# Splitting the opening loads of a GEGLU kernel over two DMA queues: transposes on SyncE, weights on ScalarE

## The chip, the cores and the metric

One core of a Trainium2 chip runs the kernel. The metric is device time in microseconds (us), lower is better. The runs of the kernel before lie between 275.07 and 275.65 us. Each run is marked fast or slow by its time against the fastest of the same kernel; ratios use fast runs alone.

Names of engines: PE is TensorE (matrix products), PEld its weight loads, DVE is VectorE, ACT is ScalarE, POOL is GpSimd, SP is SyncE. "ACTq" and "SPq" are the DMA issues of ScalarE and SyncE. The profile calls SyncE's DMA queue q1 and ScalarE's q10. A load is issued by an engine and lands when all its data have arrived; a semaphore, a counter that the load raises then, tells of it.

## The reference

```python
B, S, D, F = 32, 32, 1024, 3584          # 1024 tokens
return (gelu(x @ w_gate) * (x @ w_up)) @ w_down      # all bf16
```

## The kernel before

The kernel computes `x @ w_gate` and `x @ w_up` in chunks of 256 columns, with x transposed so that its columns lie on the partitions. The change concerns only the first 20 us, the "head", in which the first data arrive. x comes in two ways: a small piece untransposed (`x_nat`, turned on TensorE), and four DMA transposes (`load_xT`). The weights come as plain loads. `DT` is 8 tiles of 128 along D, `KD` is 4 and `KQ` is 2.

```python
load_nat(nc.sync, 0, 0, HALF)
load_nat(nc.scalar, 0, HALF, NB_P)
...
load_ahead(0, 0, 1)                       # a12a rows k0: 128 KB of w_gate, SyncE
load_nat(nc.scalar, 1, 0, NB_P)
load_ahead(0, 1, 2, nc.scalar)            # a12a k1
for which, eng in enumerate((nc.sync, nc.scalar)):
    load_w(eng, 0, which, KD, KD + KQ)    # wg and wu d4-5
load_xT(0, KD + KQ, DT)                   # T1: 256 KB transpose
load_ahead(0, KQ, KD)                     # a12a k2-3: 256 KB
load_w0(nc.sync, KD + KQ, DT)             # wg, wu d6-7: 128 KB each
load_ahead(1, 0, KD)                      # second a12a: 512 KB
load_xT(0, 0, KD)                         # T2: 512 KB transpose
load_w0(nc.sync, 0, KD)                   # wg, wu d0-3: 256 KB each
load_xT(1, 0, KD)                         # T3: 512 KB transpose
load_xT(1, KD, DT)                        # T4: 512 KB transpose
```

TensorE uses them in this order:

```python
# a12a k0-1 (psC/psA), then:
plain0(tok0, KD, KD + KQ)                 # wg, wu d4-5
for j, copy in enumerate((nc.scalar.copy, nc.vector.tensor_copy) * 2):
    product_ahead(ps[j], 0, j, KQ)        # a12a k2-3 and T1
    copy(ahead[0][:, j, :], ps[j])
plain0(tok0, KD + KQ, DT)                 # wg, wu d6-7
...                                       # chunk 1's loads are issued
for j, tag in enumerate("CCAA"):
    product_ahead(ps, 1, j)               # second a12a
    ...
# then wg, wu d0-3 with T2, later T3 and T4
```

The framework gives every load one of eight semaphores in turn, and a load waits until the load that had its semaphore before has landed. The traces show such waits (before: 0.3 us of SyncE for `x_nat`, ahead of wu d6-7).

Of the kernel before, what the change touches and what calls it, by code (L numbers as in the profile page):

```python
# [13 lines left out]
def kernel(  # L14
# [20 lines left out]
    nc = tc.nc  # L35
# [13 lines left out]
    DT, FT = D // P, F // P  # L49
    KD = DT // 2  # L50
# [3 lines left out]
    KQ = DT // 4  # L54
# [76 lines left out]
    def load_w(eng, ci, which, d0, d1):  # L131
        f0 = ci * FC * P
        src = (wg_r, wu_r)[which]
        eng.dma_start(out=w_tiles[ci, which][:, d0:d1, :], in_=src[:, d0:d1, f0 : f0 + FC * P])
# [54 lines left out]
    with tc.manual_schedule():  # L189
# [12 lines left out]
        def load_ahead(i, k0, k1, eng=nc.sync):  # L202
            f0, n = FC + i * KB, min(KB, NAHEAD - i * KB)
            eng.dma_start(
                out=a12_ahead[i][:, k0:k1, : n * P],
                in_=wg_r[:, KD + k0 : KD + k1, f0 * P : (f0 + n) * P],
            )

        def load_w0(eng, d0, d1):
            for which in (0, 1):  # L210
                load_w(eng, 0, which, d0, d1)

        def load_xT(nb, d0, d1):
            t = ((b11, b12), (b21, b22))[d0 // KD][nb]
            nc.sync.dma_start_transpose(
                out=t[:, d0 % KD : (d1 - 1) % KD + 1, :], in_=xf[nb * NB : (nb + 1) * NB, d0 * P : d1 * P]
            )
# [3 lines left out]
        load_ahead(0, 1, 2, nc.scalar)  # L221
        for which, eng in enumerate((nc.sync, nc.scalar)):
            load_w(eng, 0, which, KD, KD + KQ)
        load_xT(0, KD + KQ, DT)
        load_ahead(0, KQ, KD)
        load_w0(nc.sync, KD + KQ, DT)
        load_ahead(1, 0, KD)
        load_xT(0, 0, KD)
        load_w0(nc.sync, 0, KD)
        load_xT(1, 0, KD)  # L230
        load_xT(1, KD, DT)

# [17 lines left out]
        def plain(ps, which, fl, nb, d0, d1, first=0, last=DT - 1):  # L250
            for dt in range(d0, d1):
                nc.tensor.matmul(  # L252
                    ps,
                    lhsT=w_tiles[0, which][:, dt, fl * P : (fl + 1) * P],
                    rhs=x_rows(dt, nb),
                    start=(dt == first),
                    stop=(dt == last),
                )
# [24 lines left out]
        def product_ahead(ps, i, j, k0=0, k1=KD, cols=slice(None)):  # L283
            for k in range(k0, k1):
                nc.tensor.matmul(  # L285
                    ps[:, cols],
                    lhsT=a12_ahead[i][:, k, j * P : (j + 1) * P],
                    rhs=b21[:, k, cols],
                    start=(k == 0 and not cols.start),
                    stop=(k == KD - 1),  # L290
                    skip_group_check=True,
                )
# [4 lines left out]
        def plain0(tok0, d0, d1):  # L297
            for which in (0, 1):
                for dt in range(d0, d1):
                    for fl in range(FC):  # L300
                        plain(tok0[fl][which], which, fl, 0, dt, dt + 1, KD, KD - 1)
# [11 lines left out]
        for j, copy in enumerate((nc.scalar.copy, nc.vector.tensor_copy) * 2):  # L313
            product_ahead(ps[j], 0, j, KQ)
            copy(ahead[0][:, j, :], ps[j])
        plain0(tok0, KD + KQ, DT)
        a12_ahead.append(xpool.tile([P, KD, (NAHEAD - 2 * KB) * P], bf16, name="a12b"))
        load_w_all(1, 1)
# [297 lines left out]
```

## Time and profile before

| what | before | where it is read |
|---|---|---|
| time | 275.38 us, median of 3 | runs |
| span, PE busy | 273.3 us, 267.9 us | page, engines |
| DMA wait of PE in the head | 0.54 us, at 4.45 us | timeline of PE |
| DMA rate, 4 to 8 us and 8 to 12 us | 279 and 288 GB/s | table of windows |

Two lines of the page of the kernel before: the busy time of PE with its share of the span, and the chain of work that ended last, by engine.

```profile
PE 267.9 (98%) x1190; PEld 188.9 (69%) x1206; DVE 196.6 (72%) x196; ACT 110.8 (41%) x181; POOL 108.3 (40%) x55
...
PE 97%; DMA 1%; issue 0%; ACT 0%; SPq 0%
```

TensorE is the bound, from its first product to the end. A wait of TensorE in the head goes straight into the total.

The timeline of PE before, at the first use of each later load (start in us, duration, engine, line, operation, output and inputs, shape, count). A bracket at the end would name a wait.

```profile
8.48 1.03 PE L285 MATMUL psC<-b,a12a 128*128 128x512 bf16 x4
...
10.21 0.81 PE L252 MATMUL psA<-b,wg 128*128 128x512 bf16 x3
11.07 1.03 PE L252 MATMUL psB<-b,wu 128*128 128x512 bf16 x4
11.94 1.89 PE L285 MATMUL psC<-b,a12a 128*128 128x512 bf16 x8
...
15.39 1.03 PE L252 MATMUL psA<-b,wg 128*128 128x512 bf16 x4
16.25 1.03 PE L252 MATMUL psB<-b,wu 128*128 128x512 bf16 x4
...
25.75 1.89 PE L270 MATMUL psA<-b,wg 128*128 128x512 bf16 x8
```

No bracket: nothing is waited for. The DMA view of the kernel before, asked for single issues, gives size and time from issue to landing. Here are a12a k2-3 (issued at 3.60 us), wg d6-7 (4.21), the second a12a (5.44) and T2 (5.96).

```profile
a12a<-in_w_gate_dram SPq DMA_DIRECT2D x1, 256.0 KB, 4.5
...
wg<-in_w_gate_dram SPq DMA_DIRECT2D x1, 128.0 KB, 4.3
...
a12a<-in_w_gate_dram SPq DMA_DIRECT2D x1, 512.0 KB, 5.1
...
b<-in_x_dram SPq DMA_TRANSPOSE x1, 6.2
```

Issue plus landing time gives 8.1, 8.5, 10.5 and 12.2 us, each ahead of its use (8.48, 10.21, 11.94 and, for T2, 15.39 us). The table of windows before, for 4 to 8 us and 8 to 12 us (stretch, length, busy time of PE, PEld, DVE, ACT and POOL, granted clock, DMA share, GB/s):

```profile
4.00:8.00 4.00, 3.55 (x26) 2.55 (x27) 0.74 (x4) 0.12 (x1) 0.00 (x0) 1.00 1.22 279
8.00:12.00 4.00, 3.95 (x19) 1.83 (x19) 1.38 (x2) 1.17 (x2) 0.00 (x0) 1.00 1.13 288
```

The DMA engines are at full share.

### The profile page before, as it was taken

What the parts mean: (1) busy time and instruction counts of PE and PEld (TensorE: products, weight loads), DVE (VectorE), ACT (ScalarE), POOL (GpSimd) and SP (SyncE); (2) the same over time, 40 slices, a digit from 0 to 9 for tenths busy, and PEclk for the clock granted to TensorE, in tenths of its full rate; (3) what the DMA queues carried; (4) which work ended last, traced back from release to release, by engine and by line L of the source; (5) the groups of instructions that cost most, each with busy time, mean ns of one, the idle gap of its engine ahead of it and who ended that gap; (6) DMA issues with size and microseconds to landing.
All of it is one profiled execution on the core that took longest, in us unless ns stands there. A gap on an engine that the chain in (4) does not pass through costs nothing.

```text
span 273.3 us, 3350 instructions
## 1 busy us (share of the span) xinstructions
PE 267.9 (98%) x1190; PEld 188.9 (69%) x1206; DVE 196.6 (72%) x196; ACT 110.8 (41%) x181; POOL 108.3 (40%) x55
## 2 busy tenths in 40 slices
PE   8999999999999999999999999999999999999995
PEld 4444777877778676676868686754447888888883
DVE  1269996877756676776667576568999999999611
ACT  1271664554643646455563636430300032972001
POOL 1000099997897694949576684000000000000000
PEclk9999999999999999999999999999999999999999
DMA  7994321414505405050514280004992254786202
GB/s 166 290 251 105 111 75 40 117 42 113 156 11 143 137 19 155 0 153 0 156 28 126 79 269 1 0 2 132 329 342 83 93 175 163 240 279 203 78 0 78
DMA packets 53841, 33.77 MB, mean 124 GB/s; under 512 B 9792, under 2 KB 53824, under 8 KB 53824
## 3 DMA queue, kind: packets, MB, share of 16 engines
q1 hardware_dynamic: 50304, 31.00, 39.3%
q10 hardware_dynamic: 3520, 2.56, 2.9%
q8 instruction: 9, 0.15, 0.3%
q14 instruction: 8, 0.07, 0.1%
HBM read 29.62 MB, written 2.10 MB: 116 GB/s over the span
## 4 chain that ended last, share of the span: by engine, by line
PE 97%; DMA 1%; issue 0%; ACT 0%; SPq 0%
PE psA L270 34%; PE psA L446 18%; PE psC L270 17%; PE psC L446 7%; PE psB L446 7%; PE psB L270 5%; PE psB L252 3%; PE psA L252 2%; PE psC L285 2%; PE psA L285 1%; DMA a12a<-in_w_gate_dram 1%; ACT o_sb L586 0%; SPq L191 0%; PE tp L243 0%
## 5 line engine op out<-in xcount | busy, mean ns | idle before, releaser
L270 PE MATMUL psA<-t,s 128*128 128x512 f32 x208 | 54.2, 402 | 0.0
L262 ACT ACTIVATE h<-c 128x512 bf16<-128x512 f32 x52 | 31.6, 627 | 36.6 <-DVE c L350 36.6
L270 PEld LDWEIGHTS psA<-t,s 128*128 128x128 f32 x208 | 39.1, 188 | 9.2
L168 POOL TENSOR_TENSOR s<-wu 128x1024 fp32r<-128x1024 bf16 x12 | 27.4, 2285 | 23.7 <-PE psC L270 12.8
L350 DVE TENSOR_TENSOR c<-sn,psA 128x512 f32<-128x512 f32 x26 | 17.8, 684 | 16.8 <-PE psA L270 16.8
L270 PEld LDWEIGHTS <-wg 128*128 128x128 bf16 x168 | 15.4, 98 | 20.1 <-issue 3.4
L169 POOL TENSOR_TENSOR s<-s,wg 128x1024 fp32r<-128x1024 f32 x12 | 27.7, 2312 | 0.9
L171 POOL TENSOR_TENSOR s<-wg,wu 128x1024 fp32r<-128x1024 bf16 x12 | 26.6, 2216 | 0.0
L355 ACT COPY sn<-psA 128x512 f32<-128x512 f32 x42 | 23.6, 584 | 6.8 <-PE psA L270 6.8
L355 ACT COPY sn<-psC 128x512 f32<-128x512 f32 x26 | 15.2, 588 | 26.9 <-PE psC L270 22.8
L270 PE MATMUL psA<-t,a22r 128*128 128x512 f32 x104 | 25.9, 391 | 0.0
L270 PE MATMUL psC<-t,s 128*128 128x512 f32 x104 | 25.8, 390 | 0.0
L270 PE MATMUL psC<-b22r,s 128*128 128x512 f32 x104 | 25.7, 389 | 0.0
L270 PE MATMUL psA<-b,wg 128*128 128x512 bf16 x100 | 24.1, 379 | 0.2
L270 PEld LDWEIGHTS psC<-t,s 128*128 128x128 f32 x104 | 19.4, 188 | 4.4 <-ACT ahead L377 0.3
L270 PEld LDWEIGHTS psA<-t,a22r 128*128 128x128 f32 x104 | 19.5, 188 | 4.1
L270 PEld LDWEIGHTS psC<-b22r,s 128*128 128x128 f32 x104 | 19.5, 188 | 4.1
L350 DVE TENSOR_TENSOR c<-sn,psC 128x512 f32<-128x512 f32 x26 | 17.7, 688 | 5.5 <-PE psC L270 5.5
L369 DVE TENSOR_TENSOR hi<-h,psA 128x512 bf16<-128x512 bf16 x14 | 9.6, 689 | 12.5 <-PE psA L270 12.5
L425 DVE TENSOR_TENSOR hi<-c,h 128x512 bf16<-128x512 f32 x14 | 18.0, 1284 | 0.5
L425 DVE TENSOR_TENSOR lo<-c,h 128x512 bf16<-128x512 f32 x12 | 17.8, 1479 | 0.6
L170 POOL TENSOR_TENSOR s<-wg,s 128x1024 fp32r<-128x1024 bf16 x8 | 17.3, 2156 | 0.6
(94 smaller groups left out, 396.9 us busy)
## 6 DMA issues: line engine op xcount, KB each, us to landing
wdb<-in_w_down_dram SPq DMA_DIRECT2D x12, 512.0 KB, 5.0
wu<-in_w_up_dram SPq DMA_DIRECT2D x11, 512.0 KB, 4.0
wdb<-in_w_down_dram SPq DMA_DIRECT2D x12, 384.0 KB, 4.7
wg<-in_w_gate_dram SPq DMA_DIRECT2D x6, 512.0 KB, 5.1
wg<-in_w_gate_dram SPq DMA_DIRECT2D x10, 256.0 KB, 4.4
v<-in_w_down_dram SPq DMA_DIRECT2D x4, 512.0 KB, 6.7
out_dram<-o_sb ACTq DMA_DIRECT2D x16, 128.0 KB, 1.7
v<-in_w_down_dram SPq DMA_DIRECT2D x4, 384.0 KB, 7.6
```

The lines of the kernel that those rows point to most:

```text
L168: yield eng.tensor_tensor(s1, a21, a22, ADD)
L169: yield eng.tensor_tensor(s2, s1, a11, SUB)
L170: yield eng.tensor_tensor(s4, a12, s2, SUB)
L171: yield eng.tensor_tensor(s3, a11, a21, SUB)
L252: nc.tensor.matmul(ps, lhsT=w_tiles[0, which][:, dt, fl * P : (fl + 1) * P], rhs=x_rows(dt, nb), start=(dt == first), stop=(dt == last),)
L262: nc.scalar.activation(h, src, ACT.Gelu_apprx_tanh)
L270: nc.tensor.matmul(ps, lhsT=lhs[:, k, :], rhs=rhs[:, k, :], start=(start and k == 0), stop=(k == KD - 1), skip_group_check=True,)
L350: tt(t, s, ps, ADD)
L355: nc.scalar.copy(t, ps)
L369: tt(g_of(ft)[:, :NB], h0, psa, MUL)
L425: tt(g_of(ft)[:, NB:], added(sn5[fl], psa[fl]), h1[fl], MUL)
L446: nc.tensor.matmul(banks[m], lhsT=lhs(k)[:, m * P : (m + 1) * P], rhs=rhs(k), start=(start and k == 0), stop=(k == HF - 1), skip_group_che ...
```

## The change

Its intent: after its first three loads SyncE issues only the transposes of the head, whose issue is long, and the weights no longer queue behind them. ScalarE, idle early on, issues the weights.

```diff
         for which, eng in enumerate((nc.sync, nc.scalar)):
             load_w(eng, 0, which, KD, KD + KQ)
+
         load_xT(0, KD + KQ, DT)
-        load_ahead(0, KQ, KD)
-        load_w0(nc.sync, KD + KQ, DT)
-        load_ahead(1, 0, KD)
+        load_ahead(0, KQ, KD, nc.scalar)
+        load_w0(nc.scalar, KD + KQ, DT)
+        load_ahead(1, 0, KD, nc.scalar)
         load_xT(0, 0, KD)
-        load_w0(nc.sync, 0, KD)
         load_xT(1, 0, KD)
         load_xT(1, KD, DT)
...
             product_ahead(ps[j], 0, j, KQ)
             copy(ahead[0][:, j, :], ps[j])
+        load_w0(nc.scalar, 0, KD)
         plain0(tok0, KD + KQ, DT)
```

## The prediction

> **What bounds the kernel.** TensorE. The page gives PE 267.9 us busy of a 273.3 us span (98%), and the chain of waits is 97% PE. From 4.45 us on, the timeline shows no PE gap over about 0.05 us in the head. Its only DMA wait is 0.54 us for the first `a12a` rows at 4.45 us, plus start-up before it; the change touches neither. So nearly nothing can be gained: at most some 0.5 us.
>
> **What the change does.** It removes no bytes and no PE work. Five loads (`a12a` k2-3 256 KB, `wg`/`wu` 128 KB each, second `a12a` 512 KB; then `wg`/`wu` 256 KB each) move from the SyncE to the ScalarE queue. On SyncE they took 0.37 to 0.58 us of issue each; the transposes took 1.34, 4.23 and 4.96 us (for two). SyncE thus finishes its transposes some 3 us earlier (13 instead of 16.4 us) and chunk 1's weights are issued earlier. ScalarE gets about 2 us of issues in an idle stretch: its table load slips from 2.83 to about 5 us, done before its first copy at 9.12 us. The last `wg`/`wu` are issued after its copy at 9.98 us, so about 10.6 and 11.1 us against 10.23 and 10.86.
>
> **Where it touches the critical path.** In the table of 1 us windows the DMA engines are at full share from 4 to 18 us, at 180 to 350 GB/s. Before, one queue held the order of need. Issue time plus time to landing, against PE's first use:
> - `a12a` k2-3: lands 8.1, used 8.27
> - `wg` / `wu` d6-7: 8.5 / 8.9, used 9.99 / 10.86
> - second `a12a`: 10.55, used 11.72
> - first half of x (transposed): 12.2; `wg` / `wu` d0-3: 13.7 / 14.55, used 15.18 / 16.04
> - second token half: 16.6 and about 18.5, used 18.84 and 22.3
>
> Slack is only 0.2 to 1.9 us. Now 1.5 MB of transposes needed at 15 us or later are in flight beside 1 MB of weights needed before 12 us. The Trainium skill, "DMA: Bandwidth & Descriptors", section "Issuing engines are not separate DMA queues", says the DMAs of both queues run on the same 16 engines and interleave, and that a second issuer saves only issue time. The trace agrees in the one overlap it has: ScalarE's `wu` (issued 2.35) landed at 6.55, SyncE's transpose (issued 2.21) at 7.3[...].
>
> Estimate with equal shares (some 145 GB/s each, from the 290 GB/s of the windows) from 6.4 us: `a12a` k2-3 at 8.2, `wg`/`wu` at 9.0/9.9, second `a12a` at about 13.5 instead of 10.55, a stall of up to 1.8 us at 11.7 us. If weights get a bigger share (their rows are 512 or 1024 bytes, transposed rows 256), it lands near 11.8 and hardly stalls. The later `wg`/`wu` land at 15 to 17 us; a stall at 11.7 absorbs that. Lateness does not add up: the largest counts. All of it reaches the end, since PE is full afterwards. Transposes and chunk 1 weights arrive earlier, which pays nothing.
>
> **Prediction.** 276.3 us (+0.9). Range 275.0 to 278.2. Faster by over 2%: 0.01; within 2%: 0.95; slower by over 2%: 0.04.
>
> **What would show it.** PE waiting on DMA at the products of the second `a12a` (about 11.7 us) for 0.5 to 2 us, its landing time up from 5.1 to 7 us or more; transposes of the first x half landing near 10 us, not 12.2; SyncE issuing chunk 1's `wu` near 13 us; the rest of the timeline shifted by one constant; PE busy time unchanged.
>
> **What would make it wrong.** Transposes that hold up the other queue's descriptors altogether (then several us, even over 2%); weights favoured in the sharing (then no change); a ScalarE issue blocked so long that its copies come late.

## The result, and the profile after

The changed kernel took 278.25 us, median of 4 (277.94 to 278.94), beside 275.5 us for the kernel before in the same rounds. The ratio is 1.0106, with a 95% interval of 1.0083 to 1.0129. A ratio here is the mean time of one kernel's fast runs over that of the other's of the same rounds, so it is not quite the ratio of the medians. In microseconds it is 0.0106 x 275.5 = 2.9. Below, "+2.9 us" always means a ratio turned into us that way.

The same two lines of the page after:

```profile
PE 268.6 (97%) x1190; PEld 188.3 (68%) x1206; DVE 195.3 (71%) x196; ACT 110.9 (40%) x181; POOL 108.2 (39%) x55
...
PE 92%; DMA 6%; ACTq 0%; issue 0%; ACT 0%
```

PE has the same work (268.6 against 267.9 us), but the chain now holds 6% of DMA. The timeline of PE after, at the same places:

```profile
8.97 1.04 PE L285 MATMUL psC<-b,a12a 128*128 128x512 bf16 x4
...
12.34 0.82 PE L252 MATMUL psA<-b,wg 128*128 128x512 bf16 x3 [1.47 <-DMA wg<-in_w_gate_dram]
13.22 1.03 PE L252 MATMUL psB<-b,wu 128*128 128x512 bf16 x4
14.39 1.90 PE L285 MATMUL psC<-b,a12a 128*128 128x512 bf16 x8 [0.15 <-DMA a12a<-in_w_gate_dram]
...
17.86 1.03 PE L252 MATMUL psA<-b,wg 128*128 128x512 bf16 x4
19.05 1.04 PE L252 MATMUL psB<-b,wu 128*128 128x512 bf16 x4 [0.17 <-DMA wu<-in_w_up_dram]
...
28.55 1.89 PE L270 MATMUL psA<-b,wg 128*128 128x512 bf16 x8
```

Subtracting row from row gives the delay so far:

| first use of | before | after | delay so far |
|---|---|---|---|
| a12a k2-3 | 8.48 | 8.97 | 0.49 |
| wg d6-7 | 10.21 | 12.34 | 2.13 |
| second a12a | 11.94 | 14.39 | 2.45 |
| wg d0-3 | 15.39 | 17.86 | 2.47 |
| wu d0-3 | 16.25 | 19.05 | 2.80 |
| first product of chunk 1 | 25.75 | 28.55 | 2.80 |

The spans differ by 2.9 us, so nearly the whole loss (2.80 us) arises before 19.1 us. More than half of it (1.64 us) arises at wg d6-7. (A bracket counts only PE's idle time; matrix products are pipelined and their ends modelled, so the delays of starts are the better measure.)

The DMA view after, for the same four loads, now issued at 3.17 (a12a k2-3), 4.55 (wg d6-7), 5.50 (second a12a) and 3.60 us (T2):

```profile
a12a<-in_w_gate_dram ACTq DMA_DIRECT2D x1, 256.0 KB, 5.8
...
wg<-in_w_gate_dram ACTq DMA_DIRECT2D x1, 128.0 KB, 7.7
...
a12a<-in_w_gate_dram ACTq DMA_DIRECT2D x1, 512.0 KB, 8.8
...
b<-in_x_dram SPq DMA_TRANSPOSE x1, 11.0
```

They land at 8.9, 12.3, 14.4 and 14.6 us. ScalarE issued wg d6-7 and the second a12a within 0.35 us of when SyncE had issued them before (4.21 and 5.44). Nothing was won in issue time, and landing takes 3.4 to 3.7 us longer. T2, issued 2.4 us earlier than before, lands 2.4 us later. The table of windows after:

```profile
4.00:8.00 4.00, 3.34 (x25) 2.29 (x26) 0.73 (x4) 1.28 (x1) 0.00 (x0) 1.00 1.21 182
8.00:12.00 4.00, 2.73 (x12) 0.89 (x10) 1.38 (x2) 1.17 (x2) 0.00 (x0) 1.00 1.23 227
```

The engines are as busy as before (1.21 and 1.23) but move 182 and 227 GB/s, not 279 and 288. The DMA view after, for 5 to 11 us, by queue (packets, MB, share of 16 engines):

```profile
q1 hardware_dynamic: 3023, 0.77, 92.0%
q10 hardware_dynamic: 530, 0.38, 33.8%
```

SyncE's transposes got 0.77 MB through, ScalarE's more urgent weights 0.38 MB. Last, three lines of the chain of waits after, in order of time (start, length, what):

```profile
5.50 8.85 DMA a12a<-in_w_gate_dram
14.35 0.02 issue
14.37 4.63 DMA wu<-in_w_up_dram
```

ScalarE issued wu d0-3 only when the second a12a had landed, because the two have one semaphore (the trace has them under one number). I had expected that issue at 11.1 us.

One more stretch shows how the two queues were served. From 11 to 13 us SyncE's T3 (issued at 8.70 us) and ScalarE's second a12a (issued before it, at 5.50 us) were both under way. The DMA view for these 2 us, by queue:

```profile
q10 hardware_dynamic: 744, 0.55, 114.1%
q1 hardware_dynamic: 29, 0.01, 1.7%
```

The load issued later moved next to nothing. That is no fixed share per queue. Nor do transposes always start so late: in m1's stretch A, below, 0.17 MB had moved 2.1 us after the issue of the first one.

### The profile page after: what moved, and what is told of

It is laid out like the page before. It is cut to its first block, busy times and chain, and to the rows that moved or that the text cites. A ratio compares the mean times of both kernels' runs of the same rounds, so it can differ in the third digit from the quotient of the medians.

```text
span 276.2 us, 3351 instructions
## 1 busy us (share of the span) xinstructions
PE 268.6 (97%) x1190; PEld 188.3 (68%) x1206; DVE 195.3 (71%) x196; ACT 110.9 (40%) x181; POOL 108.2 (39%) x55
## 4 chain that ended last, share of the span: by engine, by line
PE 92%; DMA 6%; ACTq 0%; issue 0%; ACT 0%
PE psA L270 34%; PE psA L447 18%; PE psC L270 17%; PE psC L447 7%; PE psB L447 7%; PE psB L270 5%; DMA a12a<-in_w_gate_dram 3%; PE psB L252 2%; DMA wu<-in_w_up_dram 2%; PE psA L252 2%; DMA x_nat<-in_x_dram 1%; PE psC L285 1%; ACTq L134 0%; ACT o_sb L587 0%; ACTq L191 0%
## 5 line engine op out<-in xcount | busy, mean ns | idle before, releaser
L270 PEld LDWEIGHTS <-wg 128*128 128x128 bf16 x168 | 15.4, 98 | 20.2 <-issue 3.4
L426 DVE TENSOR_TENSOR hi<-c,h 128x512 bf16<-128x512 f32 x14 | 16.6, 1188 | 0.5
```

Of the source, the lines that this page charges most:

```text
L270: nc.tensor.matmul(ps, lhsT=lhs[:, k, :], rhs=rhs[:, k, :], start=(start and k == 0), stop=(k == KD - 1), skip_group_check=True,)
L426: tt(g_of(ft)[:, NB:], added(sn5[fl], psa[fl]), h1[fl], MUL)
```

## The experiments

The theory after the result, called F: both queues feed the same engines, and a load is served roughly by its time of issue across both. The change lets T2, needed at 15.4 us, be issued at 3.6 us, ahead of wg, wu and the second a12a (4.55 to 5.5 us), which are needed by 12 us. Part M of the theory (then F+M): transposes in flight beside plain loads of the other queue lower the total rate.

Rivals. S, from the prediction: the two queues share equally, whatever was issued first. L: the waits of ScalarE's issues for earlier landings. T: the late issue of the last wg/wu. G: any two queues lose rate. All but the three marked "wrong" are correct.

| run | what | against before, 95% interval | in us |
|---|---|---|---|
| e1_head_only | first four weight loads moved | 1.0065 to 1.0117 | +2.5 |
| e2_tail_only | last two moved | 1.0022 to 1.0062 | +1.2 |
| e3_gated | the change, T2 held back to 6 us | 1.0099 to 1.0222, unclear | see there |
| e4_one_queue_late | one queue, T2 put before wg | 1.0034 to 1.0068 | +1.4 |
| e5_gated_tail_back | e3 with the last two on SyncE | 0.9998 to 1.0044 | +0.6 |
| e6_plain_after (wrong) | the change, plain copies for transposes | 1.0108 to 1.0140 | +3.4 |
| e7_plain_before (wrong) | before, plain copies for transposes | 1.0000 to 1.0044 | +0.6 |
| m1_queues (wrong) | loads alone, by kind and queue | none | none |
| r_after_again | the changed kernel again | 1.0073 to 1.0143 | +3.0 |
| e8_merged_head | e1 with merged first loads | 1.0024 to 1.0085 | +1.5 |
| e9_merged_before | before with merged first loads | 1.0054 to 1.0113 | +2.3 |

### e1: the first four loads alone

```diff
 # against the changed kernel
         load_xT(0, 0, KD)
+        load_w0(nc.sync, 0, KD)
         load_xT(1, 0, KD)
...
-        load_w0(nc.scalar, 0, KD)
         plain0(tok0, KD + KQ, DT)
```

> Half of the change: the first four weight loads go to the ScalarE queue, the last two (wg/wu d0-3) stay on SyncE between the transposes. Theory F (order of issue: the second transpose of x, issued at 3.6 us, is served before wg, wu and the second a12a issued at 4.55 to 5.5 us): most of the loss stays, +2.0 to +2.8 us, wg d6-7 lands near 12 us. Rival T (the late issue of the last wg/wu on ScalarE at 12.8 and 14.4 us): loss gone or under +0.8 us.

It took +2.5 us, and the view of waits has this line for PE (total, times, longest):

```profile
PE psA L253 <- DMA wg<-in_w_gate_dram: 1.4, 1, 1.4
```

Wg d6-7 landed at 12.2 us. The first four loads alone bring most of the loss, as F said; T is not the main cause.

### e2: the last two loads alone

```diff
 # against the kernel before
-        load_w0(nc.sync, 0, KD)
...
+        load_w0(nc.scalar, 0, KD)
         plain0(tok0, KD + KQ, DT)
```

> The other half: the first four loads stay on SyncE ahead of the second transpose, only the last wg/wu go to ScalarE between its copies. Theory F: wg d6-7 lands near 8.5 us as before, total 0 to +0.8 us. Rival T: +1.5 us or more.

Wg d6-7 landed at 8.1 us and was not waited for. The run took +1.2 us, over the 0.8 that F allowed. Its one large wait:

```profile
PE psB L251 <- DMA wu<-in_w_up_dram: 1.2, 1, 1.2
```

That is the same fault at another place. SyncE, rid of these two loads, issued T3 at 9.9 us and T4 at 11.9 us. ScalarE's wu d0-3 came at 12.0 us, beside T4, and took 5.2 us to land instead of 3.7. One of its six runs (282.0 us) was slow. The two halves (2.5 and 1.2) do not add up to 2.9: a delay at wg d6-7 gives the later loads more time.

### e3 and e5: T2 held back

```diff
 # e3, against the changed kernel
         load_ahead(1, 0, KD, nc.scalar)
+        nc.gpsimd.tensor_copy(b11[:, 0, :1], a12_ahead[0][:, 1, :1])   # T2 overwrites this column
         load_xT(0, 0, KD)
 # e5, against e3
+        load_w0(nc.sync, 0, KD)
         load_xT(1, 0, KD)
...
-        load_w0(nc.scalar, 0, KD)
```

The copied column makes T2 wait for an early load; T2 then overwrites it, and the result is right.

> The changed kernel with one thing more: the second transpose waits (through a one-column GpSimd copy) for the second a12a row block, which landed at 6.05 us, so it is issued near 6.3 us, after ScalarE has issued wg, wu and the second a12a (4.55 to 5.5 us). The result stays right. Theory F (order of issue decides): wg d6-7 and wu land near 8.5 to 9.5 us, second a12a near 10.5 to 11.5, the 1.5 us stall is gone, total +0.2 to +1.0 us over before. Rival S of the prediction (two queues share the engines equally, whatever was issued first): transposes still take half, second a12a lands at 13 us or later, total +1.5 us or more. Rival L (the waits of ScalarE's issues for earlier landings): nothing changes, +2.5 us or more.

> The gated kernel of e3 with its last two weight loads (wg/wu d0-3) back on SyncE. Two queues remain for the first four loads, but no transpose is issued in their midst and no load of ScalarE falls beside the later transposes. Theory F+M (what hurts is a transpose issued ahead of a needed load, and transposes in flight beside loads of the other queue, which together move 160 to 210 KB/us instead of 290): both are gone, so the time is near that of before, 0 to +0.8 us, no stall over 1 us. If it stays at +1.5 us or more, the second queue hurts in a way the theory does not hold.

The total of e3 missed the expectation of F: four of its six runs were slow, 281.8 to 282.8 us, and the two counted as fast lie 4 us apart (277.6 and 281.5). The profiled run was slow, so I draw nothing from its total and leave its scatter unexplained. In e5, which keeps the gate and only takes e2's fault out, the profile is of a fast run. T2 was issued at 5.8 us, after the second a12a (5.4 us), and wg d6-7 landed at 8.3 us, the second a12a at 10.6 us, against 8.5 and 10.5 in the kernel before. The windows of e5, 4 to 8 and 8 to 12 us:

```profile
4.00:8.00 4.00, 3.91 (x27) 2.50 (x28) 0.74 (x4) 1.28 (x1) 0.19 (x1) 1.00 1.17 296
8.00:12.00 4.00, 4.00 (x21) 1.77 (x19) 1.38 (x2) 1.17 (x2) 0.00 (x0) 1.00 1.12 269
```

The rate is back at 296 and 269 GB/s, PE is busy throughout, and the time is +0.6 us with an interval that touches zero. Four weight loads still go through ScalarE. e5 is e1 with the one gating line more, and that line takes +2.5 us to +0.6. So neither the second queue as such (nor L: ScalarE's loads still wait for landings, wu d6-7 and the second a12a are issued at 5.0 and 5.4 us as in the changed kernel) costs the time; T2's place in time does. The gate has a side effect: wg d6-7 takes over another semaphore and is issued at 3.5 us, not 4.2 as in e1; wu d6-7 and the second a12a are not moved forward by it. The DMA view of e5 for 7 to 9 us, with T2 issued (5.8 us) behind these two:

```profile
q10 hardware_dynamic: 878, 0.59, 114.8%
q1 hardware_dynamic: 27, 0.00, 0.8%
```

Again the load issued later stood back. So an unequal but fixed share of the queues, a rival that I had not named, is out too. e5 is no faster than before.

### e4: the same order on one queue

```diff
 # against the kernel before
         load_ahead(0, KQ, KD)
+        load_xT(0, 0, KD)
         load_w0(nc.sync, KD + KQ, DT)
         load_ahead(1, 0, KD)
-        load_xT(0, 0, KD)
         load_w0(nc.sync, 0, KD)
```

> The kernel before with one queue kept, but the second transpose put ahead of wg d6-7, wu d6-7 and the second a12a on SyncE. Theory F: the same loss as the changed kernel without any second queue, +1.5 to +3 us, wg d6-7 lands near 12 us. Rival S or any theory in which it is the second queue that hurts: it cannot say why this should be slower; sharing absent, but FIFO order alone would also give wg late, so this run shows only how much of the loss order alone can make.

```profile
PE psC L285 <- DMA a12a<-in_w_gate_dram: 1.8, 1, 1.8
```

It took +1.4 us, slightly under the expected range, with one queue. The second a12a landed at 14.4 us, as in the changed kernel. Wg d6-7 landed at 10.6 us, not at the expected 12, so the PE wait is at another load. The way there is another too: SyncE was busy with the issue of T2 for 3.7 us, so it issued wg at 7.9 and the second a12a at 9.1 us, and the second a12a then took 5.3 us to land, hardly more than the 5.1 before. The profile is of the slowest of the six runs (277.6 us; the others 276.2 to 276.9), and its rate fell as well. The windows of e4, 4 to 8 and 8 to 12 us:

```profile
4.00:8.00 4.00, 3.91 (x24) 2.79 (x24) 0.75 (x4) 0.10 (x1) 0.00 (x0) 1.00 1.15 243
8.00:12.00 4.00, 3.95 (x19) 1.75 (x19) 1.38 (x2) 1.17 (x2) 0.00 (x0) 1.00 0.96 235
```

So T2's early place makes about half of the loss on one queue, but e4 does not separate order from rate.

### e6 and e7: no transposes at all

```diff
 # e6 against the changed kernel, e7 against the kernel before
-            nc.sync.dma_start_transpose(
-                out=t[:, d0 % KD : (d1 - 1) % KD + 1, :], in_=xf[nb * NB : (nb + 1) * NB, d0 * P : d1 * P]
-            )
+            n = d1 - d0
+            nc.sync.dma_start(
+                out=t[:, d0 % KD : (d1 - 1) % KD + 1, :].rearrange("p k (b d) -> p (k b) d", d=P),
+                in_=wd_r[:, : n * (NB // P), nb * P : (nb + 1) * P],
+            )
```

The form above fetches as many bytes of `w_down` in rows of 256 bytes.

> The changed kernel with the four transposes replaced by plain copies of the same size in rows of 256 bytes (the numbers come out wrong on purpose; instructions, queues and bytes stay). Theory M (the loss of rate needs transposes): the mixed stretch from 5 to 11 us moves over 250 KB/us, wg d6-7 lands before 10.5 us, and the excess over e7 is under 1.2 us. Rival G (any two queues beside each other lose rate, or order alone): the stretch stays near 190 KB/us and the excess over e7 is 2 to 3 us.

> Control of e6: the kernel before with the same plain copies in place of its transposes (wrong numbers on purpose). Theory M and rival G: within 0.7 us of the kernel before, no PE stall in the head over 0.6 us.

The excess of e6 over e7 is 3.4 - 0.6 = 2.8 us, as large as that of the change itself. I had expected under 1.2 us from M. The windows of e6, 4 to 8 and 8 to 12 us:

```profile
4.00:8.00 4.00, 3.22 (x25) 2.21 (x26) 0.74 (x4) 1.19 (x1) 0.00 (x0) 1.00 1.20 274
8.00:12.00 4.00, 2.80 (x14) 1.12 (x13) 0.73 (x2) 1.16 (x3) 0.00 (x0) 1.00 1.19 290
```

No rate is lost (274 and 290 GB/s; e7 has 296 and 270), and the time is lost all the same: the view of waits has 1.8 us of PE for wu d0-3 and 1.2 us at most for a12a. M is refuted as the necessary cause, and G too: two queues beside each other kept their rate. What remains in both e6 and the changed kernel is the order: loads needed late are in flight ahead of loads needed soon. But the equal size of the two losses proves little. The plain copies are quicker to issue: those in the places of T3 and T4 went out at 5.9 and 7.8 us, not at 8.7 and 14.0. And the loss lies elsewhere: wg d6-7, the main wait of the changed kernel, is not waited for in e6; about 2.0 of 3.4 us arise at wu d0-3, which was issued at 13.4 us, right after the landing of the second a12a (a wait of kind L), behind those two copies.

### m1: the loads by themselves

A program of eight stretches of loads of 512 KB each, every stretch behind the one before; T is a transpose, W weight rows of 512 bytes, K weight rows of 1024 bytes, P a plain copy with rows of 256 bytes.

```python
phases = [("A", "TT", ""), ("B", "", "WW"), ("C", "TT", "WW"), ("D", "PP", "WW"),   # SyncE, ScalarE
          ("E", "PP", ""), ("F", "TWTW", ""), ("G", "TT", "KK"), ("H", "WW", "WW")]
```

> Not the kernel but a measurement of the disputed cost: eight stretches of 1 or 2 MB of loads, each behind the one before (outputs are zeros on purpose). A: two transposes of 512 KB on SyncE alone. B: two weight loads of 512 KB (rows of 512 bytes) on ScalarE alone. C: A and B at once. D: plain copies in rows of 256 bytes on SyncE beside the weight loads on ScalarE. E: those plain copies alone. F: transpose, weights, transpose, weights on SyncE alone. G: transposes beside weight rows of 1024 bytes. H: weights on both queues. Theory M: A, B, E near 290 KB/us in their steady part; C and G well below, 160 to 220; D, F and H near 290. Rival G: D and H as low as C. If C runs near 290, the loss of rate in the kernel is no matter of the mix alone.

The windows of m1 for the steady parts of C (17 to 21 us) and G (57 to 63 us); POOL alone has work, so the columns are its busy time, granted clock, DMA share, GB/s:

```profile
17.00:21.00 4.00, 0.00 (x0) 1.00 1.16 304
...
57.00:63.00 6.00, 0.00 (x0) 1.00 1.07 241
```

A had 270, B 296, D 281, E 236, F 227 and H 296 GB/s. m1 ran once, so its state is unknown. C is as fast as A and B: transposes beside weight rows of 512 bytes lose nothing in this run. G, E and F are lower, E and F with one queue. So M does not hold in general, and why the changed kernel moved only 182 GB/s from 4 to 8 us stays open. One thing the kernel's own profiles show: in the fast ones with transposes in which T2 goes early, on two queues or one, the lower of the two windows (4 to 8 and 8 to 12 us) is 165 to 235 GB/s (changed kernel, its repeat, e1, e4, e8); where it goes late, it is 246 to 286 (before, e2, e5, e9). The slow profile of e3, with T2 late, has 203.

### r_after_again, e8 and e9: a second look, and an earlier issue

e8 and e9 merge five of the first loads into three. Fewer loads go before the four, so ScalarE's issues wait less.

```diff
 # e8 against e1, e9 against the kernel before
-        load_nat(nc.sync, 0, 0, HALF)
-        load_nat(nc.scalar, 0, HALF, NB_P)
+        load_nat(nc.sync, 0, 0, NB_P)
...
-        load_ahead(0, 0, 1)
-        load_nat(nc.scalar, 1, 0, NB_P)
-        load_ahead(0, 1, 2, nc.scalar)
+        load_nat(nc.sync, 1, 0, NB_P)
+        load_ahead(0, 0, KQ, nc.scalar)
```

> The changed kernel once more, on the chip and in the rounds of the two below, for a second profile. Every theory: +2.4 to +3.4 us over before. Order theory F: the largest PE wait in the head is again for wg d6-7 or the second a12a, and wg d6-7 again takes over 6 us from issue to landing. If the stretch from 5 to 11 us again moves only about 190 KB/us, the loss of rate belongs to this kernel; if not, it was one execution's.

> e1 (only the first four weight loads on ScalarE) with the first x and a12a loads merged from five into three, so that fewer of ScalarE's issues wait for an earlier load to land: a12a k2-3, wg, wu, second a12a should be issued by about 4 us instead of 3.1 to 5.9, before or with the second transpose (3.6 us). Theory F (order of issue decides): wg d6-7 lands before 10 us, no stall there, and the excess over e9 is under 1.2 us, where e1 had 2.5 us. Rival S (equal sharing whatever was issued first): wg still lands at 10 us or later or the second a12a after 12.5 us, and the excess stays over 1.5 us.

> Control of e8: the kernel before with the same merged first loads. Every theory: within -0.3 to +1.0 us of before (the first product may start a few tenths of a us later, since its weights come with the next row's).

The repeat of the changed kernel gave +3.0 us, with wg d6-7 taking 8.3 us to land and 165 GB/s from 4 to 8 us: the low rate is this kernel's, not one execution's. The waits moved about: the largest was now 1.6 us, for T1 and a12a k2-3, where F expected it for wg d6-7 or the second a12a. These two were issued before T2 (2.2 and 2.9 us) and landed only at 10.2 us, so order of issue does not explain that wait; the low rate may. The total did not move.

e9 missed its range: it took +2.3 us. Its first product came at 5.2 instead of 4.45 us, because the larger first loads landed later. That is 0.8 of the 1.9 us by which its profile is late at chunk 1. The other 1.1 us arise because PE itself was slower at first: from 5.6 to 7.7 us its pairs of products with a12a took 0.63 us each, where the kernel before has 0.38 from 5.45 us on, and no wait stands before them. Why is not shown. e8 took +1.5 us, so it is no slower than its control, where e1 had lost 2.5 us; F expected an excess under 1.2, S one over 1.5. But only a12a k2-3 and wg got ahead of T2 as planned; wu and the second a12a did not, and the second a12a landed at 13.4 us, where S had expected it after 12.5. The comparison of times is weakened by the late start, which gives both kernels more time for the later loads. The landing times are not. The DMA view of e8 for wg d6-7, issued at 2.37 us and so before T2 (4.44 us), and for wu d6-7, issued at 4.73 us and so just after it:

```profile
wg<-in_w_gate_dram ACTq DMA_DIRECT2D x1, 128.0 KB, 4.9
...
wu<-in_w_up_dram ACTq DMA_DIRECT2D x1, 128.0 KB, 6.3
```

They lie one behind the other on ScalarE's queue, with the same size. wg landed at 7.2 us, wu at 11.1 us. With T2 between them in time of issue, 128 KB came 3.9 us later; with equal shares of 145 GB/s it would have been an estimated 0.9 us (128 KB over 145 GB/s). The changed kernel shows the same step between a12a k2-3 (issued before T2, landed 8.9 us) and wg (issued after it, landed 12.3 us). S falls by this, and by the windows of the changed kernel (11 to 13 us) and of e5 (7 to 9 us) above.

## Why the prediction was wrong

- **That TensorE bounds the kernel, and that all lateness reaches the end: right. That nothing can be gained was not tested by itself; no run was faster than before.** PE busy is 268.6 against 267.9 us, the delay at 28.55 us is 2.80 us, that of the span 2.9 us.
- **That late transposes would compete with urgent weights: right in kind.** e5 takes the competition away and is back to +0.6 us.
- **The estimate with equal shares of 145 GB/s: the step that failed, the term for landing times.** It put wg and wu d6-7 at 9.0 and 9.9 us; they landed at 12.3 and 12.8. ScalarE's queue got 0.38 MB of 1.15 MB from 5 to 11 us, a third, and the total was 192 GB/s there, not 290. What counted in its place was the time of issue across both queues (e5 against e1, e8): T2, issued at 3.60 us, went largely before wg. From 8 to 11 us SyncE's queue moved 0.50 MB, nearly the whole of T2, and ScalarE's 0.18 MB. My evidence for equal shares was one pair of loads issued 0.14 us apart (T1 at 2.21, ScalarE's wu d4-5 at 2.35 us). Such a pair cannot tell equal shares from service by time of issue, and it does not show equal shares either: from 5 to 6 us, with both under way, SyncE's queue moved 0.13 MB and ScalarE's 0.05. And +0.9 us lay midway between equal shares (a stall of up to 1.8 us) and a bigger share for the weights (hardly any); they got the smaller one.
- **The issue times behind it: wrong.** I took it that ScalarE issues its four loads one after the other, up to 5 us. But a load waits for the landing of the load that had its semaphore before. wg was issued at 4.55 us, right after `x_nat` had landed at 4.53 and so after T2, and the last wg/wu at 12.8 and 14.4 us instead of 10.6 and 11.1. The kernel before already showed such a wait (0.3 us of SyncE for `x_nat`), and I passed over it.
- **"Lateness does not add up": held, but its last term was mis-sized.** I expected wg/wu d0-3 by 17 us and absorbed. wu's issue waited for the late second a12a, so it landed at 19.0 us and brought the delay from 2.47 to 2.80 us. One lateness was passed on to the next load through a semaphore.
- **The wait at the second a12a of 0.5 to 2 us: wrong place.** Its time to landing did rise to 8.8 us, but the main wait was 1.47 us for wg d6-7, before it (0.15 us for the second a12a).
- **T2 near 10 us, chunk 1's wu issued near 13 us: wrong.** T2 landed at 14.6 us. SyncE's four transposes took 14.2 us of issue (1.34, 5.05, 5.26 and 2.53) where I had counted 10.5, so it issued that wu at 16.57 us, against 16.42 before. Even the intended gain, an earlier free SyncE, did not come.
- **The number.** 276.3 us was said, with 278.2 as the upper end; 278.25 was measured. The sign was right; the loss of 0.9 us should have been 2.9.

What stays open: why the rate fell to 182 GB/s in the changed kernel (m1's stretch C kept 304, e6 kept 274), and so how the loss divides between order and rate. Shown is that T2's early issue brings the loss (e5 against e1) and that loads issued in the wrong order can cost as much with no loss of rate (2.8 us, e6 against e7, at other loads). e4's 1.4 us on one queue came with a lower rate. That the rate played no part in the changed kernel is not shown, and its repeat speaks against it. The scatter of e3 stays open too.

## What to carry to other kernels

Where the DMA engines are full, the one queue that issues loads in the order of need is a schedule. A second queue did not add bandwidth here (m1: 296 GB/s for the weight loads on one queue, B, and on two, H); it lets loads that are needed late start early, in front of those that are needed soon. Before moving loads to another queue, list for each its true time of issue, with the waits on earlier landings, and its deadline, and hold the late ones back if they would pass an urgent one.

## What the Trainium skill lacked or had wrong

- "DMA: Bandwidth & Descriptors", section "Issuing engines are not separate DMA queues": that DMAs of all issuers run on the same 16 engines and interleave agrees with the changed kernel, where both queues moved data from 5 to 11 us (0.77 and 0.38 MB) and took 92.0% and 33.8% of the 16 engines. The section does not say that a load waits for what the other queue issued earlier: in e8 the same 128 KB took 4.9 us when issued before the other queue's 512 KB transpose and 6.3 us when issued just after it, and landed 3.9 us later.
- The same page, section "Queues, rings and completion order": each engine goes round the queues at packet granularity. It gives no shares for packets of different size. Here ScalarE's queue, with rows of 512 and 1024 bytes, moved 0.38 MB from 5 to 11 us beside 0.77 MB of transposed rows.
- The same page, same first section, says that a second issuer saves only issue time, which is usually small beside the DMA itself. For transposes it was not small, and it was not saved: 5.05 and 5.26 us of SyncE for 512 KB each, of 11.0 and 8.5 us to landing, with the engines full.
- No page names the loss of rate seen here with transposes issued early (182 and 165 GB/s in two profiles of the changed kernel, from 4 to 8 us, against 279 before), nor when it does not occur (304 GB/s for transposes beside weight loads in m1). Its cause stays open.
- No page tells that the framework makes a load wait for the landing of an earlier one whose semaphore it takes over: wu d0-3 was issued at 14.37 us, right after the landing at 14.35 us.
